# A fused linear-attention and expert-lookup kernel: each head's first feature and each key set's first score subtracted from the others, and weight columns ordered by feature

## The chip, the cores and the metric

The kernel runs on one core of one Trainium2 chip. The metric is the device time of one execution in microseconds. The engines are TensorE (PE; its weight loads are shown as PEld), VectorE (DVE), ScalarE (ACT), GpSimd (POOL) and SyncE (SP), which only issues transfers here.

## The reference

Two results are computed from the same x (2048 rows of 512 features) and mixed by a gate. The first is linear attention with 32 heads of 16 features and a learned feature map, the second a lookup of one expert of 256 per head.

```python
def _A_ref(x, wqkv, w_phi, wo):                   # w_phi is 200 times the drawn one
    q, k, v = split of x @ wqkv                   # 32 heads of 16
    pq = einsum("bhsd,hdf->bhsf", q, w_phi);  pk = the same of k
    phi_q = concatenate([softmax(pq), softmax(-pq)])      # over the 16 features
    phi_k = concatenate([softmax(pk), softmax(-pk)])
    kv = einsum("bhsf,bhsd->bhfd", phi_k, v);  z = einsum("bhsf->bhf", phi_k)
    o = einsum(phi_q, kv) / (einsum(phi_q, z) + 1e-6)
    return o @ wo

def _B_ref(x, w_q, k1, k2, u, v):                 # 32 heads, 16 first and 16 second keys
    s1, s2 = scores of the two halves of x @ w_q against k1 and k2
    e = argmax(s1) * 16 + argmax(s2)              # one expert per head, K = 1
    g = softmax over that one score               # 1
    return sum over heads of g * gelu(x . u[e]) * v[e]

g = sigmoid((x * gate_w).sum(-1))
return g * _A_ref(x, ...) + (1 - g) * _B_ref(x, ...)
```

A softmax over a head's 16 features, and an argmax over a head's 16 scores, do not change when the same number is subtracted from all 16.

## The kernel before

The rows are cut into 16 tiles of 128 (`NT = 16`). The order of the work on every engine is written out by hand: the program text is the order of each engine's queue, and buffers come from pools with a fixed number of places. PSUM has four banks for matmul results (`mm_bank`), three for transposes and small results (`tr_bank`) and one accumulator.

Every float32 operand of the large matmuls is split in a high and a low part of the type float32r, and a product is the sum of three matmuls, high times high, high times low and low times high. `mm3` (lines 55 to 57) does this for one accumulation: with four blocks of 128 inner features it issues 12 matmuls of 512 columns into one bank. `proj` calls it for a row tile. `prod` (line 467) is the same for pairs of blocks, six matmuls.

Weights are prepared in the kernel:

- The feature map is folded into the key and query weights. `fold_k` multiplies the transposed key weights by the small matrices in `wp`, `fold_turn` turns the result and writes it with ACT copies and DVE subtractions to `wah`, `wal` (lines 243, 244) and to `kraw` (line 246); `fold_q` does it later for the query weights (lines 221, 222), into the same tiles `wah`, `wal`.
- The score weights are the query weights of the lookup times the keys in `kp` (`score_w`, line 300). Their eight parts j are turned by a transfer (`score_planes`) and joined: `join_high` (ACT, line 320) and `join_low` (POOL, line 324) write them to `sh`, `sl`. Parts 0 to 3 hold the first scores (half 0), 4 to 7 the second (half 1). All heads have their 16 columns beside each other.

Then follow two passes over the row tiles:

- The key pass. Tiles 0 to 4 and 15 go one by one (`kproj`); tiles 5 to 14 go in pairs, in which the key and value products of two tiles are computed with seven products in place of eight (`prod` with `b11`, `b21`, and with the sums `b1` to `b4`, `b22`); POOL makes the sums of x (`Sums.add`, lines 183 to 186) and their low parts (line 197). `softmax_diffs` (DVE, lines 123 to 129) reads the bank pk, subtracts each head's maximum and minimum, and writes to `d`; ACT takes exponentials (line 275), DVE sums (line 279), POOL divides (line 284), and `kvacc` (line 291) accumulates the products with the values.
- Between the passes the query weights are folded, and z is made ready by a sequence over ACT, POOL and DVE that ends in two pairs of matmuls (`z_final`, lines 938, 939).
- The query pass, `for a in range(NT - 1)`. Tile a has its query features (`front_q`, bank pq, 12 matmuls) and the next tile its scores (`front_s`, banks s, two times 12) and its products with u and the gate weights (`front_p`, bank pp, 258 columns). `softmax_diffs` reads pq. `best` (DVE, lines 736, 737) takes the maximum of each head's 16 scores and marks the places equal to it, in two halves of 512. `mid_mask` and `count` turn the marks into counts for each expert, `mid_num` and `back` compute the output (banks oT and po).

The softmax and `best` see a bank as 32 heads of 16 contiguous columns:

```python
p3 = p.rearrange("p (h f) -> p h f", f=F)
```

`count` begins with a DVE copy (line 808) that reads a small PSUM result by groups: `o.rearrange("p (g w a) -> p g a w", w=2, a=F)`, so that neighbouring elements of the read lie 16 floats apart.

Of the kernel before, what the change touches and what calls it, by code (L numbers as in the profile page):

```python
# [16 lines left out]
ALU = mybir.AluOpType  # L17
# [3 lines left out]
P = 128  # L21
S = 2048
D = 512
# [11 lines left out]
def mix_kernel(ctx, tc, xT, wqT, wkT, wv, wphi, wo, wq, kk, ug, ev, cst, out):  # L35
# [15 lines left out]

    def mm3(o, pairs, first=True, last=True):
        n = len(pairs)
        for i, (ah, al, bh, bl) in enumerate(pairs):
            pe.matmul(o, ah, bh, start=(first and i == 0), stop=False)  # L55
            pe.matmul(o, ah, bl, start=False, stop=False)  # L56
            pe.matmul(o, al, bh, start=False, stop=(last and i == n - 1))  # L57

# [56 lines left out]

    def proj(o, t, wh, wl, c0, c1, ks=range(NK)):
        mm3(o, [(*xs(t, k), wh[:, k, c0:c1], wl[:, k, c0:c1]) for k in ks], ks[0] == 0, ks[-1] == NK - 1)

    def softmax_diffs(p, d, st, step=lambda: None):
        p3 = p.rearrange("p (h f) -> p h f", f=F)  # L120
        d4 = d.rearrange("p (h s f) -> p h s f", s=2, f=F)
        mx, mn = st[:, 0:32], st[:, 32:64]
        dve.tensor_reduce(mx, p3, axis=AX.X, op=ALU.max)
        step()
        dve.tensor_reduce(mn, p3, axis=AX.X, op=ALU.min)
        step()
        dve.tensor_tensor(d4[:, :, 0, :], p3, mx.unsqueeze(2).to_broadcast([P, H, F]), op=ALU.subtract)
        step()
        dve.tensor_tensor(d4[:, :, 1, :], mn.unsqueeze(2).to_broadcast([P, H, F]), p3, op=ALU.subtract)
        step()  # L130
# [71 lines left out]

    fv = lambda a, q: a.rearrange("p k (b c) -> p (k b) c", c=P)[:, :, 32 * q:32 * q + 32]

# [3 lines left out]
    def fold_q(raw, wh, wl):  # L208
        o = four("foldq")
        for i in range(2):  # L210
            for k in (2 * i, 2 * i + 1):
                for b in range(NK):
                    for q in range(4):
                        r = slice(32 * q, 32 * q + 32)
                        c0 = (k * NK + b) * 32
                        pe.matmul(o[q][:, c0:c0 + 32], raw[r, b, k * P:(k + 1) * P], wp[r, b, :],
                                  start=True, stop=True, skip_group_check=True)
            yield
        for q in range(4):
            part = o[q].rearrange("p (g c) -> p g c", c=32)  # L220
            act.copy(fv(wh, q), part)
            dve.tensor_tensor(fv(wl, q), part, fv(wh, q), op=ALU.subtract)
        yield
# [11 lines left out]
    def fold_turn(tmp, wh, wl):  # L235
        o = four("turnk")
        for k in range(NK):
            for q in range(4):
                pe.transpose(o[k][:, q * P:(q + 1) * P], tmp[q][:, k * P:(k + 1) * P], ident)
        by_row = lambda a: a.rearrange("p (q j i) -> p q j i", q=4, j=4)  # L240
        by_head = lambda a: a.rearrange("p (j q i) -> p q j i", q=4, j=4)
        for k in range(NK):
# [27 lines left out]
    def kproj(t):  # L270
        pks[t] = mm_bank(f"pk{t}")
        proj(pks[t], t, wah, wal, 0, D)

# [41 lines left out]
    def join_tp(j, tp, tj):  # L315
        act.copy(tj.bitcast(U16).rearrange("p (k n j) -> p j k n", j=2, n=P),
                 tp.rearrange("p (j k) n -> p j k n", j=2))

    def join_high(j, tj):
        act.copy(sh[:, :, P * j:P * j + P], tj.rearrange("p (k e) -> p k e", k=NK))  # L320

    def join_low(j, tj):
        js = slice(P * j, P * j + P)
        pool.tensor_tensor(sl[:, :, js], tj.rearrange("p (k e) -> p k e", k=NK), sh[:, :, js], op=ALU.subtract)

# [6 lines left out]
    def front_s(t, half):  # L332
        e = st8[t]
        e[half] = mm_bank(f"s{half}_{t}")
        proj(e[half], t, sh, sl, 512 * half, 512 * half + 512)

# [29 lines left out]
    act.dma_start(kp, kk)  # L366
    act.dma_start(cs, cst)
    x_split(1)
    dve.tensor_tensor(t2r, rawv[:, 2:4], rawv[:, 0:2], op=ALU.subtract)
# [93 lines left out]

    def prod(o, left, right, first):
        for i, ((ah, al), (bh, bl)) in enumerate(zip(left, right)):
            for j, (x_, w_) in enumerate(((ah, bh), (ah, bl), (al, bh))):
                pe.matmul(o, x_, w_, start=(first and i + j == 0), stop=(i == 1 and j == 2),  # L467
                          skip_group_check=True)
# [8 lines left out]
    for t in range(5, NT - 1, 2):  # L477
# [14 lines left out]
        a = pks[t] = mm_bank(f"pk{t}")  # L492
        prod(a, tile_of(t, 0), b11, True)
        b = mm_bank(f"pu{t}")
# [25 lines left out]
        if t == 5:  # L520
# [7 lines left out]
            join_tp(j2, tp, tj2)  # L528
        prod(a, tile_of(t, 2), b21, False)
        k_diffs(t)  # L530
# [142 lines left out]
    def front_q(t):  # L673
        pq = mm_bank(f"pq{t}")
        proj(pq, t, wah, wal, 0, D)
        st8[t]["pq"] = pq
# [53 lines left out]
    def best(t, half):  # L730
        e = st8[t]
        if half == 0:
            e["eq"] = w2.tile([P, 1024], BF16, tag="eq", name=f"eq{t}")
        p3 = e[half].rearrange("p (h f) -> p h f", f=F)
        mx = w2.tile([P, 32], F32, tag="mx", name=f"mx{half}_{t}")
        dve.tensor_reduce(mx, p3, axis=AX.X, op=ALU.max)  # L736
        dve.tensor_tensor(e["eq"][:, 512 * half:512 * half + 512].rearrange("p (h f) -> p h f", f=F), p3,  # L737
                          mx.unsqueeze(2).to_broadcast([P, H, F]), op=ALU.is_equal)

# [538 lines left out]
```

## Time and profile before

| | |
|---|---|
| three runs, median (lowest to highest) | 367.05 us (366.94 to 367.19) |
| the profiled execution | 367.09 us |
| its span in the profile | 365.3 us |
| mean granted TensorE clock | 0.999 |
| busy: PE, DVE, ACT, POOL | 358.8, 318.5, 256.7, 206.6 us |

A row of the groups gives line, engine, operation, output and inputs by the program's names, shape and count, then the busy time, the mean length of one instruction in ns, and the idle time of the engine just ahead of them with what ended it. A row of one line's view has the shortest, median and longest duration in ns and the first and last start. A row of the timeline begins with start and length in us; in brackets stands the idle time ahead of it and what it waited for. A row of the stages gives the stretch in us from the start, its length, the busy time and instructions of PE, PEld, DVE, ACT and POOL, the granted clock, the share of the DMA engines and GB/s.

### The profile page before, as it was taken

How to read it: one execution, taken by the hardware profiler on the slowest of the kernel's cores; microseconds unless marked ns; L12 is line 12 of the kernel's file. 1: busy time of each engine (PE TensorE's matmuls, PEld its weight loads, DVE VectorE, ACT ScalarE, POOL GpSimd, SP SyncE). 2: the span in 40 equal slices, each digit the busy share in tenths (PEclk: the TensorE clock that was granted, in tenths of full speed). 3: DMA queues.
4: the chain of work that ended last, by engine and by line, in shares of the span. 5: the costliest groups of instructions: out<-in, count | busy, mean ns of one | idle time of the engine just before them, and what ended most of it. 6: DMA issues, size and time to landing. Idle time of an engine off the chain costs nothing.

```text
span 365.3 us, 8628 instructions
## 1 busy us (share of the span) xinstructions
PE 358.8 (98%) x3404; PEld 282.2 (77%) x3404; DVE 318.5 (87%) x639; ACT 256.7 (70%) x455; POOL 206.6 (57%) x205
## 2 busy tenths in 40 slices
PE   7999999999999999999999999999999999999996
PEld 3766667777778878887888888888888888888764
DVE  3679999999968889999999799699899899699791
ACT  4586577977566666695786876866769787667882
POOL 1079989988938947446337355634734635636130
PEclk9999999999999999999999999999999999999999
DMA  7868787459693112243471344263344245145233
GB/s 254 321 237 304 241 274 248 137 210 309 206 247 99 57 38 51 39 100 45 101 117 43 88 86 90 57 104 65 80 86 102 50 111 101 46 88 129 31 100 117
DMA packets 75752, 47.57 MB, mean 130 GB/s; under 512 B 67264, under 2 KB 68160, under 8 KB 73408
## 3 DMA queue, kind: packets, MB, share of 16 engines
q1 hardware_dynamic: 74848, 46.15, 46.8%
q10 hardware_dynamic: 864, 0.87, 0.9%
q8 instruction: 27, 0.44, 0.5%
q14 instruction: 13, 0.11, 0.1%
HBM read 26.43 MB, written 4.19 MB: 84 GB/s over the span
## 4 chain that ended last, share of the span: by engine, by line
PE 86%; ACT 5%; POOL 3%; DMA 2%; DVE 2%; issue 1%; SPq 0%; POOLq 0%; ACTq 0%; DVEq 0%
PE po L889 9%; PE s L55 7%; PE s L56 7%; PE s L57 7%; PE pk L467 5%; PE po L896 5%; PE pu L467 4%; PE ws L300 4%; PE pq L55 4%; PE pq L56 4%; PE pq L57 4%; PE oT L776 2%; PE kvacc L291 2%; PE pp L55 2%; PE pp L56 2%; PE pp L57 2%
## 5 line engine op out<-in xcount | busy, mean ns | idle before, releaser
L728 POOL TENSOR_TENSOR d<-d,st 128x512 f32<-128x512 f32 x30 | 32.6, 1106 | 49.3 <-DVE st L721 48.1
L699 POOL TENSOR_TENSOR w<-d,zb 128x512 f32<-128x512 f32 x32 | 41.2, 1310 | 18.7 <-ACT d L693 18.7
L55 PE MATMUL s<-sh,xh 128*128 128x512 f32 x128 | 50.4, 394 | 0.0
L56 PE MATMUL s<-sl,xh 128*128 128x512 f32 x128 | 49.9, 389 | 0.0
L57 PE MATMUL s<-sh,xl 128*128 128x512 f32 x128 | 49.8, 389 | 0.0
L757 ACT COPY pl<-d 128x1024 uint16<-128x1024 uint16 x32 | 33.3, 1046 | 18.7 <-POOL d L728 18.7
L768 ACT COPY ptb<-tp 128x1024 uint16<-128x1024 uint16 x32 | 41.7, 1370 | 0.4 <-DMA tp<-pl 0.4
L284 POOL TENSOR_TENSOR d<-d,st 128x1024 f32<-128x1024 f32 x16 | 32.6, 2036 | 8.5 <-ACT d L275 6.5
L844 POOL TENSOR_TENSOR cf<-cf,px 128x256 f32<-128x256 f32 x15 | 11.1, 741 | 33.6 <-DVE cf L840 31.8
L55 PEld LDWEIGHTS s<-sh,xh 128*128 128x128 f32 x128 | 24.0, 188 | 5.3 <-issue 0.4
L57 PEld LDWEIGHTS s<-sh,xl 128*128 128x128 f32 x128 | 24.0, 188 | 5.1
L56 PEld LDWEIGHTS s<-sl,xh 128*128 128x128 f32 x128 | 24.0, 188 | 4.8
L55 PE MATMUL pq<-wah,xh 128*128 128x512 f32 x64 | 25.2, 393 | 0.0
L57 PE MATMUL pq<-wah,xl 128*128 128x512 f32 x64 | 24.9, 390 | 0.0
L56 PE MATMUL pq<-wal,xh 128*128 128x512 f32 x64 | 24.9, 389 | 0.0
L703 DVE TENSOR_REDUCE st<-d 128x32 f32<-128x512 f32 x32 | 20.5, 678 | 3.6 <-ACT d L693 3.5
L164 DVE TENSOR_TENSOR xl<-xr,xh 128x512 fp32r<-128x512 f32 (+2 forms) x17 | 21.7, 1292 | 1.7 <-ACT xh L160 1.6
L737 DVE TENSOR_TENSOR eq<-s,mx 128x512 bf16<-128x512 f32 x32 | 22.1, 692 | 1.1
L736 DVE TENSOR_REDUCE mx<-s 128x32 f32<-128x512 f32 x32 | 21.8, 680 | 0.2 <-PE s L57 0.2
L707 DVE TENSOR_REDUCE st<-w 128x32 f32<-128x512 f32 x32 | 20.5, 676 | 0.9 <-POOL w L699 0.9
L279 DVE TENSOR_REDUCE st<-d 128x64 f32<-128x1024 f32 x16 | 19.4, 1210 | 1.8 <-ACT d L275 1.6
L927 ACT COPY ot<-po 128x512 f32<-128x512 f32 x15 | 8.7, 589 | 16.3 <-PE po L896 14.8
(271 smaller groups left out, 1097.1 us busy)
## 6 DMA issues: line engine op xcount, KB each, us to landing
wq<-wq SPq DMA_DIRECT2D x16, 1024.0 KB, 5.2
xr<-xT SPq DMA_DIRECT2D x15, 256.0 KB, 5.1
y<-ot SPq DMA_DIRECT2D x15, 256.0 KB, 2.0
rawk<-wkT SPq DMA_DIRECT2D x1, 1024.0 KB, 6.8
rawq<-wqT SPq DMA_DIRECT2D x1, 1024.0 KB, 6.8
rawu<-ug SPq DMA_DIRECT2D x2, 258.0 KB, 5.5
rawv<-wv ACTq DMA_DIRECT2D x2, 256.0 KB, 4.7
rawv<-wv SPq DMA_DIRECT2D x2, 256.0 KB, 6.0
```

The costliest lines, as they stand in the source:

```text
L55: pe.matmul(o, ah, bh, start=(first and i == 0), stop=False)
L56: pe.matmul(o, ah, bl, start=False, stop=False)
L57: pe.matmul(o, al, bh, start=False, stop=(last and i == n - 1))
L284: pool.tensor_tensor(g64(d), g64(d), b64(st[:, 128:192]), op=ALU.mult)
L467: pe.matmul(o, x_, w_, start=(first and i + j == 0), stop=(i == 1 and j == 2), skip_group_check=True)
L699: pool.tensor_tensor(hs(e["w"], i), hs(e["ph"], i), hs(zb, i), op=ALU.mult)
L728: eng.tensor_tensor(g64(d)[:, gs_], g64(d)[:, gs_], r[:, gs_].unsqueeze(2).to_broadcast([P, 32, F]), op=ALU.mult)
L736: dve.tensor_reduce(mx, p3, axis=AX.X, op=ALU.max)
L737: dve.tensor_tensor(e["eq"][:, 512 * half:512 * half + 512].rearrange("p (h f) -> p h f", f=F), p3, mx.unsqueeze(2).to_broadcast([P, H, F] ...
L757: act.copy(pl, e["ph"][:, halves[i]].bitcast(U16).rearrange("p (c j) -> p j c", j=2))
L768: act.copy(p16[:, t % 2, :, 4 * i:4 * i + 4, :], st8[t]["tp"][i].rearrange("p (j g) n -> p j g n", j=2))
L889: pe.matmul(po, a, b, start=(i == 0), stop=False)
```

## The change

Ahead of the folds POOL subtracts the first of each 16 columns of `wp` and of `kp` from the other 15 and sets the first to zero (`from_first`). All that is made of them, the folded key and query weights and the score weights, then has a zero column for the first feature of each head. The columns are put in the order feature, then head, so that the 32 zero columns of a bank stand together at its start. The second scores (half 1) are laid out as two runs of 256 columns with 16 heads each (the last 256 columns of `sh` and `sl` hold an operand of the pairs, `t4h` and `t4l`, through the key pass, while parts 4 and 5 are joined), so that there a run of 16 zero columns stands at the start of each. In each accumulation into pk, pq or s the first matmul writes all 512 columns, and the others write the 480 (half 1: two times 240) that are not zero. The pairs' other products are not touched.

The copies after the folds and the joins write the new order, `softmax_diffs` and `best` read it, and on the host the rows of the folded weights and the places in `wphi` change so that the turned result has its heads in order. The number of instructions on ACT and DVE is the same.

```diff
-    def mm3(o, pairs, first=True, last=True):
+    def mm3(o, pairs, first=True, last=True, live=lambda a: a):
         n = len(pairs)
         for i, (ah, al, bh, bl) in enumerate(pairs):
-            pe.matmul(o, ah, bh, start=(first and i == 0), stop=False)
-            pe.matmul(o, ah, bl, start=False, stop=False)
-            pe.matmul(o, al, bh, start=False, stop=(last and i == n - 1))
+            whole = first and i == 0
+            f = (lambda a: a) if whole else live
+            pe.matmul(f(o), ah, f(bh), start=whole, stop=False, skip_group_check=True)
+            pe.matmul(live(o), ah, live(bl), start=False, stop=False, skip_group_check=True)
+            pe.matmul(live(o), al, live(bh), start=False, stop=(last and i == n - 1), skip_group_check=True)
+
+    def from_first(w):
+        g = w.rearrange("p a (i f) -> p (a i) f", f=F)
+        pool.tensor_tensor(g[:, :, 1:], g[:, :, 1:], g[:, :, 0:1].to_broadcast([P, 8, F - 1]), op=ALU.subtract)
+        pool.memset(g[:, :, 0:1], 0.0)
+
+    HALF_RUNS = (1, 2)
+
+    def live_of(runs):
+        return lambda a: a.rearrange("p (r c) -> p r c", r=runs)[:, :, H // runs:]
+
+    live = lambda a: a[:, H:]
+    heads = lambda a: a.rearrange("p (f h) -> p h f", f=F)
...
     def softmax_diffs(p, d, st, step=lambda: None):
-        p3 = p.rearrange("p (h f) -> p h f", f=F)
+        p3 = heads(p)
...
-    fv = lambda a, q: a.rearrange("p k (b c) -> p (k b) c", c=P)[:, :, 32 * q:32 * q + 32]
+    fv = lambda a, q: a.rearrange("p k (f h) -> p k f h", h=H)[:, :, :, 8 * q:8 * q + 8]
...
-            part = o[q].rearrange("p (g c) -> p g c", c=32)
+            part = o[q].rearrange("p (k m f) -> p k f m", k=NK, f=F)
...
-        by_row = lambda a: a.rearrange("p (q j i) -> p q j i", q=4, j=4)
-        by_head = lambda a: a.rearrange("p (j q i) -> p q j i", q=4, j=4)
+        by_row = lambda a: a.rearrange("p (h f) -> p f h", f=F)
+        by_head = lambda a: a.rearrange("p (f h) -> p f h", f=F)
...
-        proj(pks[t], t, wah, wal, 0, D)
+        proj(pks[t], t, wah, wal, 0, D, live=live)
...
+    def places(a, j):
+        n = H // HALF_RUNS[j // 4]
+        c0, h0 = P * j // (F * n) * (F * n), 8 * j % n
+        return a[:, :, c0:c0 + F * n].rearrange("p k (e h) -> p k e h", h=n)[:, :, :, h0:h0 + 8]
+
+    by_key = lambda tj: tj.rearrange("p (k m e) -> p k e m", k=NK, e=F)
+
     def join_high(j, tj):
-        act.copy(sh[:, :, P * j:P * j + P], tj.rearrange("p (k e) -> p k e", k=NK))
+        act.copy(places(sh, j), by_key(tj))
 
     def join_low(j, tj):
-        js = slice(P * j, P * j + P)
-        pool.tensor_tensor(sl[:, :, js], tj.rearrange("p (k e) -> p k e", k=NK), sh[:, :, js], op=ALU.subtract)
+        pool.tensor_tensor(places(sl, j), by_key(tj), places(sh, j), op=ALU.subtract)
...
-        proj(e[half], t, sh, sl, 512 * half, 512 * half + 512)
+        proj(e[half], t, sh, sl, 512 * half, 512 * half + 512, live=live_of(HALF_RUNS[half]) if half else live)
...
     act.dma_start(kp, kk)
     act.dma_start(cs, cst)
+    from_first(wp)
+    from_first(kp.rearrange("p a b c -> p (a b) c"))
     x_split(1)
...
-        prod(a, tile_of(t, 0), b11, True)
+        prod(a, tile_of(t, 0), b11, True, live)
...
-        prod(a, tile_of(t, 2), b21, False)
+        prod(a, tile_of(t, 2), b21, False, live)
...
-        proj(pq, t, wah, wal, 0, D)
+        proj(pq, t, wah, wal, 0, D, live=live)
...
     def best(t, half):
-        p3 = e[half].rearrange("p (h f) -> p h f", f=F)
         mx = w2.tile([P, 32], F32, tag="mx", name=f"mx{half}_{t}")
-        dve.tensor_reduce(mx, p3, axis=AX.X, op=ALU.max)
-        dve.tensor_tensor(e["eq"][:, 512 * half:512 * half + 512].rearrange("p (h f) -> p h f", f=F), p3,
-                          mx.unsqueeze(2).to_broadcast([P, H, F]), op=ALU.is_equal)
+        r = HALF_RUNS[half]
+        n = H // r
+        p4 = e[half].rearrange("p (r f h) -> p r h f", r=r, f=F)
+        m3 = mx.rearrange("p (r h) -> p r h", r=r)
+        eq = e["eq"][:, 512 * half:512 * half + 512].rearrange("p (r h f) -> p r h f", r=r, f=F)
+        if r == 1:
+            p4, m3, eq = p4[:, 0], mx, eq[:, 0]
+        dve.tensor_reduce(m3, p4, axis=AX.X, op=ALU.max)
+        m4 = m3.unsqueeze(r > 1 and 3 or 2).to_broadcast([P, r, n, F] if r > 1 else [P, n, F])
+        dve.tensor_tensor(eq, p4, m4, op=ALU.is_equal)
```

More of the change, by code (lines that the diff above doesn't have):

```diff
@@ L114, in xs, with proj @@
         return tuple(m[:, k, :] for m in x_of(t))
-    def proj(o, t, wh, wl, c0, c1, ks=range(NK)):
-        mm3(o, [(*xs(t, k), wh[:, k, c0:c1], wl[:, k, c0:c1]) for k in ks], ks[0] == 0, ks[-1] == NK - 1)
+    def proj(o, t, wh, wl, c0, c1, ks=range(NK), live=lambda a: a):
+        mm3(o, [(*xs(t, k), wh[:, k, c0:c1], wl[:, k, c0:c1]) for k in ks], ks[0] == 0, ks[-1] == NK - 1, live)
     def softmax_diffs(p, d, st, step=lambda: None):
-        p3 = p.rearrange("p (h f) -> p h f", f=F)
+        p3 = heads(p)
         d4 = d.rearrange("p (h s f) -> p h s f", s=2, f=F)
@@ L462, in mix_kernel, with prod @@
             pool.tensor_tensor(t4l, by4(t4r), t4h, op=ALU.subtract)
-    def prod(o, left, right, first):
+    def prod(o, left, right, first, live=lambda a: a):
         for i, ((ah, al), (bh, bl)) in enumerate(zip(left, right)):
             for j, (x_, w_) in enumerate(((ah, bh), (ah, bl), (al, bh))):
-                pe.matmul(o, x_, w_, start=(first and i + j == 0), stop=(i == 1 and j == 2),
+                whole = first and i + j == 0
+                f = (lambda a: a) if whole else live
+                pe.matmul(f(o), x_, f(w_), start=whole, stop=(i == 1 and j == 2),
                           skip_group_check=True)
@@ L1247 @@
     for h in range(H):
-        j = (h % 8) * F
-        wphi[j:j + F, h // 8, j % 32:j % 32 + F] = ph[h]
+        q, b, i = h // 8, h % 8 // 2, h % 2
+        wphi[32 * q + F * i:32 * q + F * i + F, b, F * i:F * i + F] = ph[h]
+    folded = lambda a: rows(a.T.reshape(4, 4, 32, D).transpose(1, 0, 2, 3).reshape(D, D))
     wq = f(B_w_q).reshape(D, H, 2, P).transpose(2, 1, 3, 0).reshape(8, 4, 2, P, D).transpose(0, 2, 3, 1, 4)
@@ L1257 @@
         "xT": c(x.reshape(NT, P, NK, P).transpose(0, 3, 2, 1)),
-        "wqT": rows(w[:, :D].T),
-        "wkT": rows(w[:, D:2 * D].T),
+        "wqT": folded(w[:, :D]),
+        "wkT": folded(w[:, D:2 * D]),
         "wv": rows(w[:, 2 * D:]),
```

## The prediction

> **What bounds the kernel now.** I read the page first (busy time, the chain that ended last), then the timeline around one tile, and the busy time by stage.
>
> ```profile
> PE 358.8 (98%) x3404; PEld 282.2 (77%) x3404; DVE 318.5 (87%) x639; ACT 256.7 (70%) x455; POOL 206.6 (57%) x205
> ...
> PE 86%; ACT 5%; POOL 3%; DMA 2%; DVE 2%; issue 1%; SPq 0%; POOLq 0%; ACTq 0%; DVEq 0%
> ```
>
> ```profile
> 209.75 0.39 PE L55 MATMUL s<-sh,xh 128*128 128x512 f32 x1
> ...
> 218.37 0.28 PE L55 MATMUL pp<-uh,xh 128*128 128x258 f32 x1
> ...
> 219.82 0.39 PE L55 MATMUL pq<-wah,xh 128*128 128x512 f32 x1
> ```
>
> ```profile
> 21.00:49.20 28.20, 28.20 (x267) 19.03 (x265) 25.21 (x29) 19.12 (x26) 27.96 (x16) 1.00 0.76 263
> 49.20:109.00 59.80, 59.80 (x911) 43.83 (x911) 55.52 (x76) 43.00 (x60) 47.23 (x49) 1.00 0.71 227
> 109.00:133.00 24.00, 23.88 (x410) 19.70 (x409) 19.21 (x30) 15.18 (x33) 19.74 (x18) 1.00 0.36 76
> 133.00:207.00 74.00, 74.00 (x568) 60.86 (x568) 68.96 (x174) 54.51 (x109) 37.49 (x38) 1.00 0.37 71
> 207.00:320.00 113.00, 113.00 (x833) 94.38 (x832) 102.41 (x239) 84.11 (x159) 58.77 (x60) 1.00 0.38 80
> ```
>
> TensorE is the bound: 98% busy, at the full granted clock (the 1.00 of each stage row), and the chain that ended last is 86% its own. The 0.39 us of a matmul is its length through the pipeline; its price is the distance between starts. From 209.75 to 218.37 the timeline has 38 matmuls of 512 columns (24 of one tile's two score halves, 14 of po): 8.62 / 38 = 0.227 us each. From 218.37 to 219.82 stand the 12 of pp with 258 columns: 1.45 / 12 = 0.121 us. So a column costs (0.227 - 0.121) / 254 = 0.417 ns. The busy columns of the stage rows are PE, PEld, DVE, ACT, POOL: PE is full everywhere, but POOL is idle for only 0.24 us from 21 to 49.2, and DVE for 5.0 of 74 and 10.6 of 113 us in the two long stretches.
>
> **The change, part by part.** *Matmuls.* The first of each accumulation keeps 512 columns, the others write 480. Each of these saves 32 x 0.417 = 13.3 ns. How many there are:
>
> ```profile
> L55 PE MATMUL s<-sh,xh x128: 389/389/500, 115.2 to 323.8; 128*128 128x512 f32 x128
> L55 PE MATMUL pq<-wah,xh x64: 389/389/500, 124.8 to 329.2; 128*128 128x512 f32 x64
> L55 PE MATMUL pp<-uh,xh x64: 278/284/364, 127.7 to 331.0; 128*128 128x258 f32 x64
> L55 PE MATMUL pk<-wah,xh x24: 389/389/504, 18.9 to 112.5; 128*128 128x512 f32 x24
> ```
>
> ```profile
> L467 PE MATMUL pk<-wah,xh x20: 389/389/497, 45.8 to 102.4; 128*128 128x512 f32 x20
> ```
>
> Each row is one of three of its kind (L55 to L57, or the three products of L467). 12 make an accumulation and 11 of them are shortened: s 384 x 11/12 = 352, pq 176, pk 66, and in the paired key stage 55 of 60. Together 649, or 8.65 us of TensorE time. The pairs' other products (pu, pv, pe, and pk from sh) and pp stay whole. In the order of the stages: 60 until 49.2, 50 until 109, 55 until 133, 176 until 207, 275 until 320, 33 after.
>
> *What of it reaches the end.* Until 49.2 nothing does. POOL is full there, from the end of the key set-up to the operand that TensorE needs next, L197, which ends at 47.52 + 1.69 = 49.21:
>
> ```profile
> 20.94 2.38 POOL L394 TENSOR_TENSOR xraw<-xraw,xraw 128x1024 f32<-128x1024 f32 x1 [7.54 <-ACT xraw L246]
> ...
> 47.52 1.69 POOL L197 TENSOR_TENSOR xl<-xr,xh 128x512 fp32r<-128x512 f32 x1
> ```
>
> ```profile
> 60.88 0.19 PEld L467 LDWEIGHTS pe<-t1h,gl 128*128 128x128 f32 x1 [0.39 <-POOL gl L197]
> ```
>
> So 60 x 13.3 ns = 0.80 us is lost. At 60.88 the weight load waits for POOL again, and what is saved in between (11 x 13.3 = 0.15) goes too; of the 50 x 13.3 = 0.67 until 109 I keep 0.52. From 109 to 133 two parts differ:
>
> ```profile
> 120.11 2.06 ACT L221 CAST wah<-foldq 128x512 fp32r<-128x512 f32 x4 [1.92 <-PE foldq L216]
> ...
> 132.71 0.19 PEld L939 LDWEIGHTS z<-zl,neg 128*128 128x128 f32 x1 [0.43 <-DVE zl L968]
> ```
>
> From the query fold to z a chain runs over ACT, POOL and DVE (120.11 to 132.71, 12.6 us), which the change does not shorten. The 22 shortened matmuls ahead of it count (0.29 us); the 33 beside it only lengthen TensorE's wait at z, so 0.44 is lost. From 133 to 320 DVE must follow a TensorE that is 451 x 13.3 ns = 6.0 us quicker, and its idle time is 5.0 + 10.6 = 15.6 us: the 6.0 stays, less 0.25 for the place where TensorE already waits for a late DVE:
>
> ```profile
> 243.32 0.30 PEld L896 LDWEIGHTS po<-eh,cl 128*128 128x128 f32 x2 [0.42 <-DVE cl L877]
> ```
>
> After 320 DVE is the later one. It waits for tile 14's pq, and starts tile 15's without a wait, so of the last 33 x 13.3 = 0.44 us I count half:
>
> ```profile
> 319.25 0.69 DVE L123 TENSOR_REDUCE st<-pq 128x32 f32<-128x512 f32 x1 [1.54 <-PE pq L57]
> ...
> 332.23 0.68 DVE L123 TENSOR_REDUCE st<-pq 128x32 f32<-128x512 f32 x1
> ```
>
> Sum: 0.52 + 0.29 + 6.0 - 0.25 + 0.22 = 6.8 us.
>
> *Reads with a step.* With columns by feature, then head, each softmax and best-key instruction of DVE reads PSUM with a step of 32 floats (16 in score half 1); the copies after the folds and the joins read with a step of 16. Number and size of the instructions stay, so only the step can cost. The nearest rows:
>
> ```profile
> L808 DVE CAST sa<-mk x10: 211/278/282, 134.4 to 344.1; 128x128 uint16<-128x128 f32 x6, 128x64 uint16<-128x64 f32 x4
> ```
>
> ```profile
> L703 DVE TENSOR_REDUCE st<-d 128x32 f32<-128x512 f32 x32 | 20.5, 678 | 3.6 <-ACT d L693 3.5
> L279 DVE TENSOR_REDUCE st<-d 128x64 f32<-128x1024 f32 x16 | 19.4, 1210 | 1.8 <-ACT d L275 1.6
> ...
> L316 ACT COPY wtj<-wtp 128x1024 uint16<-128x1024 uint16 x8 | 10.9, 1365 | 2.3 <-POOL sl L324 1.6 <-DMA wtp<-wpl 0.7
> ...
> L305 ACT COPY wpl<-ws 128x1024 uint16<-128x1024 uint16 x8 | 8.1, 1010 | 5.1 <-PE ws L300 5.1
> ```
>
> L808 reads PSUM with a step of 16 floats already: 64 more elements cost 278 - 211 = 67 ns, 1.05 ns each; of L279 against L703, whose runs are contiguous, an element costs (1210 - 678) / 512 = 1.04. So I take 0 for DVE and ACT. The upper end is the one pair of rows in which a pattern costs something: L316 writes every second half-word, L305 reads so, 1365 against 1010 ns, or 178 ns for 512 elements. A gain is excluded: no row has an element cheaper than the contiguous one. [...]
>
> POOL's low parts now read with a step of 16 as well, for which the trace has no row:
>
> ```profile
> L324 POOL TENSOR_TENSOR sl<-wtj,sh x8: 1274/1295/1742, 40.3 to 119.1; 128x512 fp32r<-128x512 f32 x8
> ```
>
> I take 0, with 0.45 us as the upper end, the spread that this line has as it is (1742 - 1295). It counts once: the one at 40.3 lies in POOL's full stretch, and the later ones have waits of POOL behind them. [...]
>
> *Added work.* Two subtractions and two memsets on POOL, of at most 120 elements for a partition; v's memsets and the cast L392 now queue behind them and behind the landings of wp and kp.
>
> ```profile
> 13.19 0.21 POOL L392 CAST wm<-cs 128x32 bf16<-128x32 f32 x1 [11.52 <-DMA cs<-cst]
> ```
>
> POOL sat idle for 11.52 us until 13.19, waiting for cs, which the ACT queue issues after wp and kp, and its next work is L394 at 20.94; I count 0. Without that cover the key fold would start up to 0.5 us later. DMA issues stay as they are, in number and size.
>
> So the profiled execution, 367.09 us (span 365.3, and 1.8 around it; the median of the runs is 367.05), becomes 367.05 - 6.8 = **360.3 us**.
>
> **Rivals.** *A: the step costs DVE, and DVE becomes the bound (slower).* From 133 to 320 lie 112 such instructions (8 for each of 14 tiles). The gain leaves DVE 15.6 - 6.0 = 9.6 us of idle time there, so from 86 ns each DVE sets the time, and from 15.6 / 112 = 140 ns this stretch is slower than before. At 178 ns it is 19.9 - 15.6 = 4.3 us over; in the key stage 40 of them meet 4.3 us of idle time (59.8 - 55.52), 2.8 over; the tail's 12 cost some 2: **376 us**. For it: no row has a step of 32. Against it: L808.
>
> *B: TensorE is quicker, but meets others.* If the order of DVE's queue lets nothing through from 133 to 207, where it is 93% busy, 2.35 us goes, and with it half of the next stretch's 3.67: 6.8 - 4.2 leaves 2.6, **364.4 us**. For it: the wait at 243.32. Against it: it is the only such wait for DVE in 187 us, and DVE itself waits for pq as at 319.25.
>
> *C: the two runs of 240 columns in score half 1 bring nothing.* Paid as two matmuls, each is 0.121 us less 18 x 0.417 ns, 0.1135, and both are the old 0.227: 176 x 13.3 ns = 2.3 us goes, **362.6 us**. [...] Against it: 16 missing floats in 480 are little.
>
> **How the numbers follow.** Forecast 0.66, A 0.14, B 0.12, C 0.08. The low end, 358.6, has nearly all of the 8.65 us (367.05 - 8.65 = 358.4). The high end, 365.0, takes in C, B, and the upper ends of POOL and of ACT's six copies ahead of L394 (0.45 + 6 x 0.178 = 1.5 on the forecast); A is left out, and the edges of the others. The forecast's own range is 359.0 to 361.8. A measurement of this kernel can tell 0.2%, 0.7 us. Faster by more: forecast, B, C and a mild A, 0.83; within it 0.04; slower 0.13.
>
> **What would show it.** Starts of s matmuls 0.213 us apart in both halves; the softmax and best-key instructions as long as before; a longer wait at z; POOL's waits before 62 still there; DVE's idle time from the first query tile to the last smaller by some 6 us. I am wrong if these DVE instructions lengthen (A), if half 1 keeps 0.227 us (C), or if TensorE shows new waits for DVE or ACT after z (B).

## The result: 365.5 us, a quarter of the forecast gain

The changed kernel takes 365.47 us (median of 6 runs, 364.19 to 366.13) against 367.13 for the kernel before beside it (366.94 to 367.24): a ratio of 0.9948, 95% interval 0.9928 to 0.9969. It is faster, but by 1.7 us where 6.8 were forecast. Measured again later it took 364.10 us (363.39 to 365.31; 0.9928, 0.9914 to 0.9941). Its runs lie in two groups, from 363.4 to 364.3 and from 365.3 to 366.1; four of the first six lie in the upper one and one of the later six, and why is shown with the last experiments. The profiled execution is one of the lower group (364.19, span 362.5). Its busy times and its chain:

```profile
PE 353.7 (98%) x3404; PEld 281.8 (78%) x3404; DVE 319.0 (88%) x639; ACT 259.9 (72%) x455; POOL 210.8 (58%) x209
...
PE 53%; POOL 14%; DVE 14%; ACT 8%; issue 6%; DMA 3%; SPq 0%; POOLq 0%; ACTq 0%; DVEq 0%
```

TensorE's share of the chain has gone from 86 to 53%: the chain now leaves it for POOL, DVE and ACT. The pace, from the timeline around one tile (starts of the first and last shortened matmul of score half 0, half 1 and pq, ten intervals each):

```profile
209.91 0.38 PE L58 MATMUL s<-sl,xh 128*128 128x480 f32 x1
...
212.11 0.38 PE L59 MATMUL s<-sh,xl 128*128 128x480 f32 x1
...
212.56 0.38 PE L58 MATMUL s<-sl,xh 128*128 128x480 f32 x1
...
214.74 0.37 PE L59 MATMUL s<-sh,xl 128*128 128x480 f32 x1
...
219.81 0.38 PE L58 MATMUL pq<-wal,xh 128*128 128x480 f32 x1
...
221.99 0.38 PE L59 MATMUL pq<-wah,xl 128*128 128x480 f32 x1
```

They are 0.220, 0.218 and 0.218 us apart, not 0.2135. Means over the whole trace are 219, 217 and 218 ns, so a shortened matmul saves 8 to 10 ns, not 13.3: some 5.6 us over 649. The stages and the groups that answer to those of before:

```profile
21.00:49.20 28.20, 27.83 (x267) 18.98 (x265) 25.16 (x30) 19.62 (x27) 27.87 (x16) 1.00 0.82 258
49.20:109.00 59.80, 58.83 (x906) 42.79 (x906) 55.91 (x76) 44.57 (x59) 47.62 (x49) 1.00 0.70 224
...
133.00:207.00 74.00, 73.24 (x569) 61.18 (x570) 69.17 (x173) 55.24 (x111) 37.69 (x38) 1.00 0.36 71
207.00:320.00 113.00, 113.00 (x844) 96.55 (x844) 104.54 (x245) 86.38 (x164) 59.36 (x60) 1.00 0.42 85
```

```profile
L769 DVE TENSOR_TENSOR eq<-s,mx 128x512 bf16<-128x512 f32 x32 | 22.1, 691 | 1.1
L345 POOL TENSOR_TENSOR sl<-wtj,sh 128x512 fp32r<-128x512 f32 x8 | 12.8, 1606 | 0.0
L138 DVE TENSOR_REDUCE st<-pq 128x32 f32<-128x512 f32 x16 | 10.9, 684 | 4.6 <-PE pq L59 4.5
L342 ACT CAST sh<-wtj 128x512 fp32r<-128x512 f32 x8 | 8.9, 1107 | 1.1 <-PE pk L492 1.0
```

The rows of the trace before that answer to the last three of these:

```profile
L324 POOL TENSOR_TENSOR sl<-wtj,sh 128x512 fp32r<-128x512 f32 x8 | 10.8, 1348 | 0.0
L123 DVE TENSOR_REDUCE st<-pq 128x32 f32<-128x512 f32 x16 | 11.0, 684 | 5.6 <-PE pq L57 5.6
L320 ACT CAST sh<-wtj 128x512 fp32r<-128x512 f32 x8 | 5.0, 624 | 1.1 <-PE pk L467 1.0
```

TensorE was full in all four stages and now lacks 0.37 us of 28.2, 0.97 of 59.8 and 0.76 of 74. DVE's stepped reads of PSUM take what they took (684 ns for the reduction of pq, 684 before; 691 for the marks of the scores, 692 before). The two joins, which read the buffer `wtj` with a step, take longer: ACT's high part 1107 ns in place of 624, POOL's low part 1606 in place of 1348. Where TensorE's weight loads wait:

```profile
49.65 0.19 PEld L492 LDWEIGHTS pu<-uh,xl 128*128 128x128 f32 x1 [0.69 <-POOL xl L212]
...
61.68 0.19 PEld L492 LDWEIGHTS pe<-t1h,gl 128*128 128x128 f32 x1 [0.91 <-POOL gl L212]
...
75.13 0.19 PEld L492 LDWEIGHTS pe<-t1h,gl 128*128 128x128 f32 x1 [0.67 <-POOL gl L212]
...
133.59 0.19 PEld L970 LDWEIGHTS z<-zl,neg 128*128 128x128 f32 x1 [0.54 <-DVE zl L999]
...
202.08 0.27 PEld L829 LDWEIGHTS <-et 128*128 128x128 bf16 x8 [0.63 <-DMA et<-eq]
```

The wait at 61 has grown from 0.39 to 0.91, and those at 75 and 202 are new. The 202 one is for the transposed equality marks of tile 5 (`turn_eq`), which the mask product reads. How the wait at 61 comes about is in the timeline ahead of it:

```profile
57.23 1.12 ACT L342 CAST sh<-wtj 128x512 fp32r<-128x512 f32 x1
...
59.62 0.64 ACT L206 CAST gh<-xr 128x512 fp32r<-128x512 f32 x1
...
60.34 1.29 POOL L212 TENSOR_TENSOR gl<-xr,gh 128x512 fp32r<-128x512 f32 x1 [0.64 <-ACT gh L206]
```

ACT's longer join stands ahead of `gh` in its queue, POOL's `gl` (the low part that belongs to `gh`) waits for `gh`, and TensorE for `gl`.

### The profile page after: what moved, and what is told of

The parts are those of the page before. It is cut to its first block, busy times and chain, and to the rows that moved or that the text cites. A ratio compares the mean times of both kernels' runs of the same rounds, so it can differ in the third digit from the quotient of the medians.

```text
span 362.5 us, 8632 instructions
## 1 busy us (share of the span) xinstructions
PE 353.7 (98%) x3404; PEld 281.8 (78%) x3404; DVE 319.0 (88%) x639; ACT 259.9 (72%) x455; POOL 210.8 (58%) x209
## 4 chain that ended last, share of the span: by engine, by line
PE 53%; POOL 14%; DVE 14%; ACT 8%; issue 6%; DMA 3%; SPq 0%; POOLq 0%; ACTq 0%; DVEq 0%
PE po L920 7%; PE s L57 4%; PE s L59 4%; PE s L58 4%; PE po L927 4%; PE pu L492 3%; PE pk L492 3%; POOL d L299 3%; PE pq L57 2%; PE pq L58 2%; PE pq L59 2%; PE ws L315 2%; PE oT L807 2%; DMA rawv<-wv 2%; ACT ptb L799 1%
## 5 line engine op out<-in xcount | busy, mean ns | idle before, releaser
L57 PE MATMUL s<-sh,xh 128*128 128x480 f32 (+1 forms) x128 | 49.5, 387 | 0.0
L58 PE MATMUL s<-sl,xh 128*128 128x480 f32 x128 | 48.6, 380 | 0.0
L59 PE MATMUL s<-sh,xl 128*128 128x480 f32 x128 | 48.6, 380 | 0.0
L57 PE MATMUL pq<-wah,xh 128*128 128x512 f32 (+1 forms) x64 | 24.6, 385 | 0.0
L179 DVE TENSOR_TENSOR xl<-xr,xh 128x512 fp32r<-128x512 f32 (+2 forms) x17 | 22.9, 1362 | 1.8 <-ACT xh L175 1.7
L58 PE MATMUL pq<-wal,xh 128*128 128x480 f32 x64 | 24.4, 381 | 0.0
L59 PE MATMUL pq<-wah,xl 128*128 128x480 f32 x64 | 24.3, 380 | 0.0
L958 ACT COPY ot<-po 128x512 f32<-128x512 f32 x15 | 8.7, 589 | 14.8 <-PE po L927 13.3
```

What stands on the lines that cost most here:

```text
L57: pe.matmul(f(o), ah, f(bh), start=whole, stop=False, skip_group_check=True)
L58: pe.matmul(live(o), ah, live(bl), start=False, stop=False, skip_group_check=True)
L59: pe.matmul(live(o), al, live(bh), start=False, stop=(last and i == n - 1), skip_group_check=True)
L179: dve.tensor_tensor(l[:, ks], rawx[t][:, ks], h[:, ks], op=ALU.subtract)
```

## The experiments

**One half of the change at a time.** Each shortens, or reorders, alone.

```diff
 # layout_only (changed kernel)
-    live = lambda a: a[:, H:]          # and live_of likewise
+    live = lambda a: a
 # short_only (kernel before): mm3, prod, proj, front_s as in the change; heads,
 #   folds, joins as before, no from_first
 # joins_plain (changed kernel): join_high, join_low
-        act.copy(places(sh, j), by_key(tj))
+        act.copy(sh[:, :, P * j:P * j + P], tj.rearrange("p (k e) -> p k e", k=NK))
```

> The changed kernel with its 649 matmuls back at 512 columns: the new order of columns, the subtraction on POOL and the copies with steps stay. My theory: the new order by itself costs time ahead of z, because the copies of the scores' weights between buffers now read with a step (the changed kernel's trace: ACT's high part 1106 ns where it was 624, POOL's low part 1554 to 1606 where it was 1295, 8 of each), and TensorE's waits for POOL around 50, 61 and 75 us grow with them: about 368.3 us, 1 to 1.5 over the kernel before, with TensorE's starts 0.227 us apart again. Rival (POOL's low parts are only later because TensorE is earlier; the order costs nothing): 367.1, no change.

> The kernel before with the same 649 matmuls written at 480 columns, at the same places of their accumulations; the old order of columns, no subtraction, no copies with steps (32 of 512 columns of these products are left out, so their values are not the reference's). My theory: without the stepped copies the waits ahead of z stay those of before, and 5.8 us of shortened matmuls less some 1.4 that lies beside full POOL and beside the chain to z is kept: about 362.7 us. Rival (the waits ahead of z come from TensorE's lead alone, whatever the order of columns): 365.5, like the changed kernel. Both: starts 0.217 to 0.220 us apart, not the forecast's 0.213.

> The changed kernel with only the high and low parts of the scores' weights (8 copies on ACT, 8 subtractions on POOL) written and read in one contiguous run, as before (the scores' columns then are not in the order that the later steps take them for). My theory: ACT's copy is back at about 624 ns and POOL's at about 1295, the wait at 62 us falls from 0.65 to about 0.4, and the time is 364.2 us, about 1 below the changed kernel. Rival (the stepped copies are covered): 365.5, no difference from the changed kernel.

The order alone: 368.30 us, 1.0038 (1.0024 to 1.0052), 1.3 slower. The shortening alone: 362.53 us, 0.9879 (0.9866 to 0.9892). The changed kernel with plain joins: 362.45 us, the same ratio. So everything that the order costs is in the 16 join instructions: new column order in the folds, stepped reads of PSUM, the subtraction on POOL and its memsets cost nothing that can be measured. I had expected 364.2 for the last, from a median of 365.5 that has runs of the upper group in it; the four runs of joins_plain have none. The lead over the kernel before, by the start of the same matmul in both traces (us; minus is earlier):

| matmul of before at | 20.0 | 48.0 | 50.1 | 60.3 | 62.0 | 75.6 | 131.4 | 133.7 | 200.0 | 210.0 | 361.3 |
|---|---|---|---|---|---|---|---|---|---|---|---|
| changed | +0.11 | +0.10 | +0.39 | +0.29 | +0.80 | +1.27 | +0.57 | +0.88 | -0.62 | -0.07 | -2.81 |
| layout_only | +0.19 | +0.19 | +0.43 | +0.42 | +0.90 | +1.37 | +1.47 | +1.40 | +1.42 | +1.42 | +1.39 |
| short_only | -0.03 | -0.62 | 0.00 | -0.11 | -0.07 | -0.09 | -1.00 | -0.62 | -2.09 | -1.57 | -4.31 |
| joins_plain | -0.52 | -1.10 | -0.50 | -0.62 | -0.58 | -0.59 | -1.50 | -1.08 | -2.57 | -2.03 | -4.84 |

(At 20.0, where hardly a matmul has been shortened yet, the four already lie 0.7 us apart, from +0.19 to -0.52; why is not shown.) The matmuls alone lose 0.6 at 49, 0.4 at z and 0.5 at 201; with stepped joins another 0.2 to 0.3 at 49 and 0.5 each at 61 and 75, and there layout_only loses the same without a single shortened matmul. So the order causes those waits, not TensorE's lead. (The changed kernel has no gain at 48 because in this run TensorE waited for a transfer of wq at 44.38, where its lead goes from -0.38 to +0.14. joins_plain and the later pool_later have no such wait, and pool_later stands at +0.31 at 50.1 all the same.)

**Which step, and is it the step.** Two kernels take one of the two stepped reads away.

```diff
 # step_high_only: POOL's first operand         # step_low_only: ACT's operand
-  by_key(tj)
+  tj.rearrange("p (k e m) -> p k e m", k=NK, e=F)
```

> The changed kernel in which POOL's low part reads its first operand in one run, ACT's high part still with the step (the low parts are then taken from the wrong places). If ACT's +0.48 and POOL's +0.26 us add up along one chain (the low part waits for the high part), 0.48 / 0.74 of the 3.0 us that both steps cost stay: 364.5 us. Rival (only ACT's step matters, because POOL's share is covered): 365.5. Rival (only POOL's matters): 362.5.

> The mirror of the one before: ACT's high part reads in one run, POOL's low part with the step. Chain of both: 0.26 / 0.74 of 3.0 us, 363.5 us. Rival (only ACT's matters): 362.5. Rival (only POOL's matters): 365.5. POOL's low part at 1.55 us or more in this kernel, at 1.3 us in the one before, would show that the step and not the earlier arrival makes it longer.

Their joins, ACT's step kept, then POOL's:

```profile
L346 POOL TENSOR_TENSOR sl<-wtj,sh 128x512 fp32r<-128x512 f32 x8 | 10.8, 1355 | 0.0
...
L342 ACT CAST sh<-wtj 128x512 fp32r<-128x512 f32 x8 | 8.8, 1102 | 1.1 <-PE pk L493 1.0
```

```profile
L345 POOL TENSOR_TENSOR sl<-wtj,sh 128x512 fp32r<-128x512 f32 x8 | 12.8, 1604 | 0.0
...
L342 ACT CAST sh<-wtj 128x512 fp32r<-128x512 f32 x8 | 5.0, 624 | 1.1 <-PE pk L492 1.0
```

Each engine pays for its own step: 0.48 us on ACT (77%), 0.25 on POOL (18%). Writing `sh` and `sl` in runs of 8, and POOL's reading of `sh` so, cost nothing (1355 and 624 have these, and the kernel before has 1348 and 624). The medians are 364.24 (0.9931, 0.9911 to 0.9952) and 363.42 (0.9912, 0.9893 to 0.9932), near the figures that I gave for adding along one chain. That is partly luck: the 3.0 us that I shared out have the two groups in them, and so have these medians. By the lower groups alone the two steps cost 0.9 and 0.6 us over joins_plain, together the 1.5 to 1.8 of the changed kernel's lower group, so they do add.

**Can the step be put elsewhere.** Into the first copy of the join, to the writing side of ACT's high part (beside other edits, below), into the matmuls' operand, or out of the way by an order by pairs of heads, which comes with the small weights and needs no step, but makes 16 runs of 30.

```diff
 # order_in_first_copy: join_tp, twice, one half-word each; joins then plain
+  act.copy(tj.bitcast(U16).rearrange("p (k e m j) -> p j k m e", j=2, k=NK, e=F)[:, b],
+           tp.rearrange("p (j k) (m e) -> p j k m e", j=2, e=F)[:, b])
 # step_in_matmul: sh, sl in the old order; the moving operand of s
+  a.rearrange("p (h f) -> p f h", f=F)[:, 1:]
 # by_pairs: wphi, kk packed by feature, then head of the pair; no step in any copy
+  live = lambda a: a.rearrange("p (g c) -> p g c", c=32)[:, :, 2:]
```

> The changed kernel with the new order made one step earlier, in ACT's copy that puts the transposed half-words together (now two copies of half the size, reading runs of 16-bit words with a step of 16 words); the high and low parts are then read in one run. My theory, if it is 4-byte reads with a step that cost: high back at 624, low at 1295, the first copy some 0.2 us longer for the second instruction, about 363 us. Rival (a step costs wherever it stands): the first copies grow by 0.5 us or more together and the time stays at 364.5 to 365.5.

376.53 us, 1.0259. (The expectation has the side wrong: as the diff shows, this copy reads one run and writes half-words 16 half-words apart.) The joins are back at 622 and 1404 ns, but the first copy is ruinous, 2575 ns for half of what took 1370:

```profile
L332 ACT COPY wtj<-wtp 128x512 uint16<-128x512 uint16 x16 | 37.3, 2575 | 3.1 <-DMA wtp<-wpl 2.3 <-POOL sl L346 0.8
```

> The whole reference, with another order of columns: by pair of heads, then feature, then head of the pair. That order comes with the small weights already (the two heads of a pair share 32 columns of wphi and kk), so the fold copies and the joins are contiguous, and the first features are left out as 16 runs of 30 of 32 columns. My theory (the loss ahead of z is that of the stepped joins, and TensorE pays for written columns, not for runs): starts 0.217 to 0.220 us apart, joins 624 and 1295 ns, about 362.5 us, as in the two kernels that had no stepped joins. Rival (each run has a price of its own, which two runs were too few to show): starts 0.227 or more, 367 us or above.

> The whole reference: the scores' high and low weights stay in the old order, copied in one run as in the kernel without stepped joins; the new order is made by the matmuls of the scores, which read their moving operand with a step of 16 (one element of each head, feature after feature) and write one run (half 0) or two (half 1). My theory: if TensorE's price for 16 runs of 30 (0.231 us between starts, where one run of 480 takes 0.218) lies on the writing side, or in the jump from run to run, a uniform step may cost nothing: 0.218 between starts and 362.5 us. Rival (the reading of the operand is what the runs cost): every element is then its own run of one, starts at 0.231 or far more apart, 369 us or above.

368.57 us (1.0043, 1.0030 to 1.0056) and 433.88 us. My theory that TensorE pays for columns alone fell in both. Score half 0, first and last shortened matmul, ten intervals each, in the order by pairs and with the step in the operand:

```profile
183.98 0.39 PE L58 MATMUL s<-sl,xh 128*128 128x480 f32 x1
...
186.28 0.39 PE L59 MATMUL s<-sh,xl 128*128 128x480 f32 x1
```

```profile
184.70 0.59 PE L59 MATMUL s<-sl,xh 128*128 128x480 f32 x1
...
188.77 0.58 PE L60 MATMUL s<-sh,xl 128*128 128x480 f32 x1
```

0.230 and 0.407 us: 16 runs of 30 take as long as 512 columns, and 480 elements each 16 floats apart nearly twice as long.

**What a matmul's price hangs on.** Two kernels, with one run each, change places and sides (other products are formed).

> The changed kernel with the shortened matmuls still 480 columns wide, but in other places: po's query product pq reads and writes the first 480 of 512; score half 0 reads the first 480 and writes the last 480; score half 1 reads the last 480 and writes the first 480, both in one run (so the products of other columns are formed). What the 5 ns between the 213.5 that 32 columns less would give and the 217 to 220 of the changed kernel hang on: if on where the operand or the result starts (32 columns in), pq goes to 213 and the halves differ from one another; if it is the width alone, all stay at 217 to 220 ns.

In other places nothing moves: pq 217, half 0 217, half 1 219 ns.

> The changed kernel with the two sides of the matmul set apart (so other products are formed): score half 0 reads with a step of 16 and writes one run of 480; score half 1 reads 16 runs of 30 and writes one run of 480; pq reads one run and writes 16 runs of 30; the unpaired pk has 448 columns in one run. If the runs cost on the reading side: half 1 0.231, pq 0.218; on the writing side: half 1 0.218, pq 0.231; on both: both above 0.218. pk with 448 columns: 0.200 by the old column price from the forecast's 0.227, or about 0.209 if each 32 columns save the 9 ns that the first 32 did.

Score half 1 (reads 16 runs, writes one) and pq (reads one, writes 16 runs):

```profile
184.22 0.39 PE L60 MATMUL s<-sl,xh 128*128 128x480 f32 x1
...
186.55 0.39 PE L61 MATMUL s<-sh,xl 128*128 128x480 f32 x1
...
190.60 0.38 PE L60 MATMUL pq<-wal,xh 128*128 128x480 f32 x1
...
192.78 0.38 PE L61 MATMUL pq<-wah,xl 128*128 128x480 f32 x1
```

0.233 and 0.218: the runs cost on the reading side alone, 12 to 15 ns for 16 of them, and one write in 16 runs is as good as in one. pk with 448 columns starts every 203 ns (median of 61 intervals), between the two figures I gave. With 512: 227, 480: 218, 448: 203, 258: 121, the price is not a straight line; the first 32 columns bring 9 ns, the next 32 bring 15. Why is not shown.

**The wait at 202.**

```diff
 # mask_later: turned(a)
-            if masks:
+            if masks and a != 5:
                 mid_mask(*masks)
             back_some(due(a) - ran)
+            if masks and a == 5:
+                mid_mask(*masks)
```

> The changed kernel with one order changed: in the step of query tile 5, the masks of tiles 4 and 5 (which wait for the transposed equality bits of tile 5) come after po's matmuls of that step instead of ahead of them. My theory: TensorE's wait of 0.54 us at 201 us is that transfer, which DVE's best-key step of tile 5 releases late, and has work to put in front: the lead that is lost from 201 to 203 us (0.62 to 0.70) stays, about 364.8 us. Rival (DVE is late by as much anyway, and the wait comes back at its next product): 365.5, no change.

363.47 us (0.9904, 0.9891 to 0.9917). The wait is gone and does not come back: the lead at 210 is 0.04 us more than at 200 (-0.99, -0.95), where the changed kernel loses 0.55 between the two. The time is 1.3 us below the figure that I gave, and that is not the masks' doing: all four runs lie together (363.26 to 363.56), and against the changed kernel's lower group, near 363.9 to 364.2, the masks are worth 0.5 to 0.7.

**Why two groups of runs.** The one run with matmuls in other places had taken 365.68 us, and its trace has a long DVE instruction that the changed kernel's has not. The kernel before, the changed kernel, then that one:

```profile
109.74 2.50 POOL L284 TENSOR_TENSOR d<-d,st 128x1024 f32<-128x1024 f32 x1
109.75 0.69 DVE L164 TENSOR_TENSOR xl<-xr,xh 128x512 fp32r<-128x512 f32 x1 [0.24 <-ACT xh L160]
```

```profile
110.85 0.69 DVE L179 TENSOR_TENSOR xl<-xr,xh 128x512 fp32r<-128x512 f32 x1 [0.21 <-ACT xh L175]
110.91 2.44 POOL L299 TENSOR_TENSOR d<-d,st 128x1024 f32<-128x1024 f32 x1
```

```profile
110.82 1.94 POOL L301 TENSOR_TENSOR d<-d,st 128x1024 f32<-128x1024 f32 x1
110.83 2.48 DVE L181 TENSOR_TENSOR xl<-xr,xh 128x512 fp32r<-128x512 f32 x1 [0.24 <-ACT xh L177]
...
113.36 0.19 PEld L61 LDWEIGHTS pk<-wah,xl 128*128 128x128 f32 x1 [1.65 <-DVE xl L181]
```

One of the two runs at its own length (0.69 or 1.94), and the other is longer by most of the time for which that one still runs beside it (by 0.56 for 0.70, 0.50 for 0.63 and 1.79 for 1.93 us). Two kernels, in which POOL starts later or earlier, and a second measurement of the changed one test it; two more kernels join it with the masks:

```diff
 # pool_later: three more memsets of ones ahead of POOL's k_mult(13)
 # pool_earlier: the two memsets of v_tile(14), v_tile(13) put behind k_mult(13)
 # mask_and_pool: pool_later and mask_later together (it tests both losses at once)
 # mask_pool_write: that, and ACT's high part walks (k, m, e): reads one run, writes with a step
```

> The changed kernel with three more small memsets on POOL (each some 0.1 us, rewriting ones that stand there) ahead of its last multiplication of the paired key stage, so that POOL starts it some 0.3 us after DVE's low part of x tile 15 instead of within 0.06 us of it. My theory: which of the two starts first decides whether DVE's instruction takes 0.69 or 2.48 us, and that alone splits the changed kernel's runs; all runs then lie in the lower group, within 0.5 us of one another, at about 364.2 us. Rival (the two groups come from somewhere else, for instance from the transfers at 43 or 201 us): still two groups, median 365.5.

> The changed kernel once more, on the chip and beside the runs of the others of this set. My theory: two groups again, at 364.2 and at 365.3 to 366.1, and in a profile of the upper group DVE's low part of x tile 15 takes some 2.5 us and is followed by a wait of TensorE of some 1.2 us; in one of the lower group it takes 0.69. Rival: the groups don't go with that instruction.

> The changed kernel with the two memsets of v that stand on POOL ahead of its last multiplication of the paired key stage (0.22 us, at 110.77) put behind it, so that the multiplication starts some 0.1 to 0.2 us ahead of DVE's low part of x tile 15 (110.85) in every run. My theory: DVE's instruction then takes some 2.5 us in place of 0.69, TensorE waits 1.2 us for it at 112, and all runs are in the upper group, 365.3 to 366.1 us. Rival (the groups have nothing to do with it): two groups again with a median like the changed kernel's beside it, 364.1 to 365.5, or the time of the lower group, 364.

> The changed kernel with both: the masks of tiles 4 and 5 after po's products in the step of tile 5, and POOL's three small memsets. The stepped joins stay. My theory: both are losses of their own, 364.2 less the 0.7 of the masks: 363.4 us, in one group of runs.

> The one before with ACT's high part walked in the other order: it reads its operand in one run and writes with a step (32 floats for half 0, 16 for half 1). POOL's low part keeps its stepped read. If the step costs on the reading side only: 624 ns again, and some 0.5 to 1 us is gained: 362.4 to 363 us. If a stepped write costs as much or more: 1106 ns or above, 363.4 us or slower; the half-words written with a step, which took 2575 ns for 512 elements, speak for this.

With POOL later all five runs lie from 363.63 to 364.39. The changed kernel again had one of six at 365.31 and five from 363.39 to 364.30; its profile is of the lower group, DVE 0.69, so no run of the upper group was profiled. With POOL earlier all five runs are the upper group, 365.04 to 365.97, and the trace shows why:

```profile
109.07 3.83 POOL L299 TENSOR_TENSOR d<-d,st 128x1024 f32<-128x1024 f32 x2 [6.18 <-ACT d L290]
...
111.06 2.39 DVE L179 TENSOR_TENSOR xl<-xr,xh 128x512 fp32r<-128x512 f32 x1 [0.24 <-ACT xh L175]
...
113.50 0.19 PEld L59 LDWEIGHTS pk<-wah,xl 128*128 128x128 f32 x1 [1.57 <-DVE xl L179]
```

So the groups are that race, and losing it costs 1.3 us (365.34 against 364.08). In the rows of the changed kernel, of the one with other places and of pool_earlier the one that starts first keeps its length, and the other takes longer (2.44 us in place of 1.94; 2.48 and 2.39 in place of 0.69). In those of the kernel before POOL's recorded start is the earlier one, by 10 ns, and yet POOL is the longer one (2.50). By what the two hold each other up is not shown.

Why the changed kernel loses the race in some runs is not shown. DVE starts 50 to 60 ns ahead in the profiles of short_only, joins_plain and mask_later too, and none of their four runs each stands apart from the others.

The two combinations take 363.39 us (0.9906, 0.9891 to 0.9920) and 363.14 (0.9901, 0.9888 to 0.9914), one group each; the first is no faster than mask_later alone, which had no run of the upper group to lose. A stepped write costs ACT what the stepped read did:

```profile
L342 ACT CAST sh<-wtj 128x512 fp32r<-128x512 f32 x8 | 9.0, 1126 | 1.1 <-PE pk L492 1.0
```

**The waits ahead of 80 us, with the stepped joins in place.**

```diff
 # pool_order (mask_pool_write): k_mult(2) behind Sums.low(5); Sums.high(7, (0,)) ahead of
 #   join_high(j2); at t == 7, k_mult(behind) behind Sums.low(9)
```

> The last version (masks later, POOL's three memsets, ACT's step on the writing side; the whole reference, stepped joins) with three instructions moved in their queues: POOL's multiplication of key tile 2 after the low part that TensorE waits for at 49 us; ACT's high part gh ahead of the score join that delays it at 57 us; POOL's multiplication of tile 6 after the low part that TensorE waits for at 75 us. My theory: the three waits of TensorE (0.6 to 0.75, 0.65 and 0.4 us more than none) are the losses ahead of 80 us and nothing stands behind them: 363.1 less 1.5, about 361.6 us. Rival (the next late operand takes their place, or the chain to z eats it, as it ate 0.4 in the kernels without stepped joins): 362.6 to 363.1.

363.04 us (0.9901, 0.9885 to 0.9918): the rival was right. The wait at 49 went as expected (lead -1.15 at 50.1, where the kernel without this has -0.17) and so did the one at 75, but one at 60 stays, and a wait for a transfer of wq at 78.5, where 0.75 us of lead goes, takes the place of the other:

```profile
PE ws L315 <- DMA wq<-wq: 0.5, 1, 0.5
PE pe L493 <- POOL gl L212: 0.5, 1, 0.5
```

What makes that transfer late was not followed. This one and mask_pool_write are faster than the kernel before and than the changed one: 0.9901 of the kernel before, where the changed one has 0.9948 and 0.9928. Between the two there is no measurable difference.

## Why the prediction was wrong

Right were: what bounds the kernel; all that is gained until 49.2 is lost there (short_only has no lead left at 50.1); a longer wait at z (0.54, was 0.43); DVE's, and the fold copies', stepped reads of PSUM cost nothing (684 and 601 ns, 684 and 600 before), so rival A is out; score half 1 is no dearer than half 0 (217 ns, 219), so rival C is out; the added subtractions cost nothing (joins_plain has them and takes 362.45 us, short_only has none and takes 362.53). DVE's idle time in the two long stretches fell, to 4.8 and 8.5 us from 5.0 and 10.6, but by 2.3 and not 6: the lead grew by 3.4 us there (+0.88 at 133.7, -2.53 at 319).

Wrong were:

1. *"I take 0" for the joins.* They cost ACT 0.48 and POOL 0.25 us, eight times each, and 1.5 to 1.8 us of the time (the changed kernel's lower group against joins_plain; the 3.0 between their medians have the race of point 4 in them). The failing argument was L808: a stepped read of PSUM stood for a stepped read of SBUF. The only row with a pattern in SBUF, L316 against L305, gave 178 ns, a third of ACT's price; and "it counts once" did not hold, since ACT's join at 57 stands in front of `gh` and POOL's at 70 in front of `gl`.
2. *"Each of these saves 32 x 0.417 = 13.3 ns."* It is 8 to 10, so 5.6 us in all and not 8.65; these 3.0 us are the largest of the misses. The slope was taken between 258 and 512 columns; at 480 the line does not hold.
3. *"The 6.0 stays, less 0.25"* is rival B in little: at 201 the lead had passed DVE's best-key step of tile 5, and 0.55 us went into the wait for its marks. The wait at 243 that I charged for is gone instead. It came through a transfer and not through an operand of DVE; in the trace before no weight load waits for that transfer, so the waits did not show how little it had to spare.
4. *Not priced at all:* the race of POOL and DVE at 110.8, 10 ns apart by the trace before and 60 after, and by their times lost in five of the changed kernel's twelve runs. It is 1.3 us in those, and most of the difference between the two measurements of the changed kernel.

The matmuls alone come to 362.5, 4.4 us less than the kernel before. Points 2 and 3 account for that: at 8.7 ns in place of 13.3 the forecast's four gains come to 4.6, and 0.55 goes at 201, which leaves about 4.1. The joins (1.5 to 1.8) and, in its upper group, the race (1.3) make it 365.5.

## What to carry to other kernels

A gain on the bounding engine that asks for a new layout is paid by the engines that make the layout; price each of these copies from a row with the same memory and the same step, and if there is none, let the range reach far: a step cost 18% on POOL and 77 to 80% on ACT here, and nearly four times the time for ACT's half-words (5.0 ns each, 1.34 before). Shorten a matmul by columns that leave one run of the operand, or two (0.217 to 0.220 us here), not by many holes in it (0.230 to 0.233 with 16 runs), and take the price between neighbouring sizes. Look for instructions of POOL and DVE that start close together ahead of the bounding engine: here one such pair, 10 to 60 ns apart, fell either way from run to run, and a few small instructions ahead of POOL's kept all five runs in the lower group.

## What the hardware showed that I had not expected

- A matmul's holes cost in the moving operand and not in the result: 16 runs of 30 read 0.230 to 0.233 us, written 0.218; 480 elements read 16 floats apart 0.407.
- ACT's step of 16 or 32 floats in SBUF costs 77 to 80% on either side, in PSUM nothing (the fold copies of `wah` 601 ns, 600 before); half-words written 32 bytes apart take 5.0 ns each (2575 / 512), where written 4 bytes apart they took 1.34 (1370 / 1024).
